# A new hand-written order, engine choice and memory map for two layers of state-space model and two of long convolution, on one core

## The chip, the cores and the metric

The kernel runs on one core of a Trainium2 chip. A core has TensorE (PE, matrix products, with a separate row for its weight loads, PEld), VectorE (DVE), ScalarE (ACT), GpSimd (POOL) and SyncE (SP). Every engine takes its instructions in the order in which they were written for it, and waits for others through semaphores. Products land in PSUM, eight banks of 512 fp32 columns on 128 partitions; everything else lives in SBUF. Transfers are issued from the SP queue, and the first small parameters from ScalarE's.

The metric is the device time of one execution in microseconds. Before the change three runs took 341.73 to 342.29 us, median 342.02.

## What is computed

Four residual layers in turn on `x`, 2048 tokens of 640 features, bf16 in and out: A, B, A, B. A normalizes, runs a diagonal complex recurrence and projects back. B normalizes and multiplies with a long convolution of `kv`. The weights are the same in both A layers, and `k`, `v` and the filter the same in both B layers.

```python
def _A_ref(x, ...):                       # x is the layernorm of the stream
    Lam_bar = jnp.exp(dt * Lam)           # 640 complex poles
    B_bar = ((Lam_bar - 1.0) / Lam)[:, None] * Bmat
    Bu = jnp.einsum("bld,pd->blp", x + 0j, B_bar)
    for t in range(L):
        h = Lam_bar[None, :] * h + Bu[:, t, :]
    y = 2.0 * jnp.einsum("blp,dp->bld", hseq, Cmat).real + x * Dskip
def _B_ref(q, k, v, shift_k, ssm_k, ssm_D):
    kv = k_shift * v                      # k_shift: 4 taps over time
    y = irfft(rfft(pad(kv)) * rfft(pad(ssm_k)))[:S] + kv * ssm_D
    return q * y
x = x + A(ln(x)); x = x + B(ln(x)); x = x + A(ln(x)); x = x + B(ln(x))
```

## The kernel before

**Tasks and their order.** The program is cut into 896 named tasks. Each has a function that emits its instructions, the tasks it depends on, and one or two engines that can do it. The text `ORDER` names every task once; `Sched.run` walks through it and emits one task after the other. So the order in the text, filtered by engine, is the order of each engine's queue. A suffix `/a`, `/d` or `/p` picks ScalarE, VectorE or GpSimd where a task has a choice; without one it runs on its first engine. `PLACE` gives every SBUF buffer its offset in one arena (in units of 64 bytes per partition, 3216 of them) and every product its PSUM bank. A buffer that lies where another lay before makes its writer wait until the earlier users are done.

**Convolution tables and kv.** `yt_*` make sine tables (`yt_io` and `yt_f0` counters on GpSimd, `yt_ph`, `yt_f2`, `yt_neg` on VectorE, `yt_sin`, `yt_f3` on ScalarE; `yt_Ci`, `yt_Si` are transposes by DMA). `kv_*` make the shifted product: small parameters come by `kv_kd`, `kv_dsl` (and `a_pl` for layer A) on ScalarE's queue, `kv_k0`, `kv_d0` and `a_p0` cast them (L1164, L1178, L359), `kv_ds` build diagonal matrices on GpSimd, `kv_lk` and `kv_lv` load k (transposed) and v, `kv_mm` is the product (L1227), `kv_ev` multiplies by v (L1243, VectorE), `kv_pd` fills 16 columns with zeros.

**Convolution, five groups of 128 features (`yq0` to `yq4`).** The filter (`kl`, stages `KA`, `KB`) and kv (`vl`, a transpose by DMA, stages `VA`, `VB`) are transformed by products (`:m`, L1272 and L1294 to L1296) that are evicted from PSUM by a copy (`:e`, ScalarE L290 or VectorE L292). `pw` multiplies the spectra on VectorE (L1350 to L1354), `IB` (L1376), a DMA transpose `tt` and `IA` (L1404) go back, and `st` writes the result to a scratch in HBM, from which `B1l` and `B2l` read it.

**Layer A's weights.** `a_ldB`, `a_ldC` load, `a_b0`, `a_b1`, `a_ct`, `a_w1` are products, `a_b0e`, `a_b1e`, `a_wc`, `a_wm`, `a_w1e` their evictions. `a_p*`, `a_t*`, `a_f`, `a_dd`, `a_lm2`, `a_lamd`, `a_tq` and `a_rq` make poles, rotation tables and diagonals. Two neighbouring tokens (four in the last chunk) are taken as one step of the recurrence.

**Layers, four chunks of 512 tokens.** For `A1c0` to `A2c3`: layernorm statistics (`ln_bn` on VectorE in A1, `ln_sq` on ScalarE elsewhere), normalization (`id`, ScalarE L696 or VectorE L698), a transpose by DMA (`tu`, L726), input products `bq` (L750) and `bp` (L765) in three groups with evictions `eq` and `ev`, then on VectorE a rotation `ri` (L803, L804), the scan `sc` (L820), the carry `cy` to the next chunk, and the rotation back `ro`. `hx` (L875) takes away the input again for the even tokens. Four output products `cp:0` to `cp:3` (L901) follow; `cp:1` and `cp:3` need `ro` alone, `cp:0` and `cp:2` need `hx` as well. `xe` adds the residual (VectorE L911, or ScalarE L909, where an identity product has added it). The last chunk has further steps: `e2`, `b4` (L781, L783) before the rotation, `h1` (L858 to L861), `eh` and two `hx` behind it. `B1` and `B2`: normalization `u`, product `mm` (L959), sum `m` (L980, L982), in B2 with a store `st`. B2's last chunk goes by single quarters (`B2c30` to `B2c33`, L944, L948).

The scans carry from chunk to chunk, and each chunk goes through A1, B1, A2, B2, so the chunks run staggered, with the convolution groups and the weights in between.

Of the kernel before, what the change touches and what calls it, by code (L numbers as in the profile page):

```python
# [59 lines left out]
a_ldB1 yt_io8 kv_pd0/p yt_ph8 a_ldB0 yq0_kl kv_kd kv_dsl a_pl yt_f0 yt_h0 kv_k0 kv_pd1/p kv_lk0 kv_lv0 yq1_kl yt_sin8  # L60
xl0 kv_lk1 kv_lv1 yt_f2 kv_pd2/d yt_f3 a_p0 a_ti yt_io0 yt_ph0 yt_f4 kv_d0 yt_neg8 yt_h1 warm a_p1 a_p2 yt_sin0
a_b00:3 a_b0e0:3/d a_b01:2 a_b00:2 kv_k1 kv_k2 yq0_ka a_b01:3 a_b0e1:2/a a_p3 a_b0e0:2/d a_b0e1:3/d a_b00:1 yq0_KA:m0
a_b00:4 a_p4a yq0_KA:e0/a a_dd yt_neg0 kv_d1 kv_d2 kv_ds0 kv_ds4 kv_ds1 yq0_KA:m3 a_p5a a_b0e0:1/a a_b0e0:4/d
yq0_KA:e3/a a_b01:0 yq0_KA:m2 a_b0e1:0/a a_b00:0 yq0_KA:m1 yq0_KA:e2/a a_p4 yq0_KA:e1/d a_b0e0:0/d a_ta kv_mm0:1
a_b01:4 a_p5b a_b0e1:4/a yt_h2 kv_ds2 kv_ds3 yt_h3/p kv_mm0:0 kv_ev0:1 kv_pd3/d yq1_ka yq1_KA:m1 yq0_KB:m2 yq0_KB:m0
yq1_KA:e1/a yq0_KB:e2/a a_t0 kv_ev0:0 A1c0_ln_bn:1/d a_p6 a_lamd/d kv_pd4/p a_f yq0_vl a_ldC0 yt_Ci a_ldC1 yq0_KB:e0/a
yt_Si kv_lv3 kv_lk2 kv_lv2 xl2 yq2_kl yq1_KA:m3 yq1_KA:m2 yq0_KB:m3 yq1_KA:e2/a yq0_KB:e3/a kv_mm1:0 yq1_KA:e3/a
a_b01:1 a_b0e1:1/d kv_ev1:0 kv_mm1:1 kv_ev1:1 a_t1 a_b11:3 a_b1e1:3/d yq0_VA:m2 a_b11:0 yq0_VA:e2/d A1c0_ln_bn:2/d
a_b1e1:0/d a_b10:1 a_b11:1 a_b1e0:1/a a_b1e1:1/a yq0_KB:m1 yq0_KB:e1/a yq0_VA:m1 a_b11:4 a_lm2 a_b1e1:4/d yq0_VA:m3
yq0_VA:e1/a yq0_VA:m0 yq0_VA:e0/a yq0_VA:e3/d yq1_KA:m0 yq1_KA:e0/a a_b10:4 a_b1e0:4/a yq0_VB:m0 a_ct1 yq0_VB:e0/a  # L70
a_wc01:0 A1c0_ln_bn:3/d yt_nci A1c0_ln_bn:0/d a_t2 yq0_VB:m3 yq0_VB:e3/a yq0_VB:m2 a_b10:2 yq0_VB:e2/a a_wm01:0 yt_nsi
# [1488 lines left out]
```

## Time and profile before

| | us |
|---|---|
| median of three runs | 342.02 |
| the profiled execution, its own time | 342.43 |
| its span, first to last instruction | 340.6 |
| VectorE busy | 320.2 (94%) |
| TensorE busy / weight loads | 309.3 (91%) / 241.8 |
| ScalarE busy | 245.1 (72%) |
| GpSimd busy | 18.1 (5%) |
| granted TensorE clock, mean | 0.979 |
| DMA: moved, mean rate | 41.61 MB, 122 GB/s |

A busy time is the union of an engine's instructions. Matmuls overlap in it, since their ends are modelled: a mean of 273 ns stands beside starts that are 109 ns apart. Evictions from PSUM and normalizations are split between VectorE and ScalarE: of the copies of 1024 columns 111 run on ScalarE and 27 on VectorE. An "idle before" is the time that the engine stood before an instruction, with the engine or transfer whose signal ended it.

### The profile page before, as it was taken

The page shows a single profiled execution, that of the slowest core. Times are in us where ns is not written, and L with a number is a line of the kernel's source. Part 1 is how long each engine was busy: PE and PEld are TensorE (multiplying, and loading weights), DVE is VectorE, ACT ScalarE, POOL GpSimd, SP SyncE. Part 2 cuts the span into 40 slices and gives each one's busy share as a digit, 9 for nine tenths or more (in the row PEclk, how much of TensorE's full clock was granted, in tenths as well). Part 3 has the DMA queues.
Part 4 walks back from the last instruction along what each step waited for, and adds up shares of the span by engine and source line. Part 5 has one row for each costly group of instructions (what it writes and reads, how often), then busy time and mean ns, then how long its engine had stood idle before and what let it go on. Part 6 is the DMA issues. An engine that isn't in the chain of part 4 may idle for free. (4 is left out here: it accounts for less than half of the span.)

```text
span 340.6 us, 8904 instructions
## 1 busy us (share of the span) xinstructions
PE 309.3 (91%) x3817; PEld 241.8 (71%) x3838; DVE 320.2 (94%) x485; ACT 245.1 (72%) x389; POOL 18.1 (5%) x52
## 2 busy tenths in 40 slices
PE   6676978967899999999999999999999899999991
PEld 2566877866788989888676678686676686775650
DVE  5999998999998699999999999999999999999995
ACT  4899987989787867774596589887385793264772
POOL 6590000000000000000000000000000000000000
PEclk9789999997999999999999999999999999999997
DMA  8988999999959293159009460624001260008013
GB/s 234 238 173 180 204 248 228 130 222 214 156 125 187 64 155 72 39 90 239 29 2 187 122 252 2 157 77 79 0 2 25 55 154 2 2 1 306 27 56 154
DMA packets 105097, 41.61 MB, mean 122 GB/s; under 512 B 97885, under 2 KB 100450, under 8 KB 105058
## 3 DMA queue, kind: packets, MB, share of 16 engines
q1 hardware_dynamic: 104912, 41.03, 56.2%
q8 instruction: 30, 0.49, 0.6%
q14 instruction: 9, 0.07, 0.1%
q10 hardware_dynamic: 146, 0.01, 0.0%
HBM read 19.02 MB, written 5.24 MB: 71 GB/s over the span
## 5 line engine op out<-in xcount | busy, mean ns | idle before, releaser
L290 ACT ACTIVATE arena<-banks 128x1024 bf16<-128x1024 f32 (+3 forms) x151 | 130.1, 911 | 54.8 <-PE banks L750 17.3
L901 PE MATMUL banks<-arena 128*128 128x128 bf16 (+1 forms) x780 | 98.2, 281 | 1.1
L901 PEld LDWEIGHTS <-arena 128*128 128x128 bf16 x800 | 59.7, 98 | 39.9 <-issue 1.7
L750 PE MATMUL banks<-arena 128*128 128x256 bf16 x400 | 46.3, 273 | 1.1 <-DVE arena L911 1.1
L765 PE MATMUL banks<-arena 128*128 128x256 bf16 x400 | 46.5, 273 | 0.0
L292 DVE CAST arena<-banks 128x1024 bf16<-128x1024 f32 (+3 forms) x39 | 41.1, 1078 | 5.5 <-PE banks L1404 2.4
L644 ACT ACTIVATE junk<-arena,sums 128x640 bf16<-128x640 f32 x48 | 39.6, 825 | 5.2 <-DVE arena L911 2.5
L750 PEld LDWEIGHTS <-arena 128*128 128x128 bf16 x400 | 38.3, 98 | 5.7 <-DMA arena<-arena 1.2
L765 PEld LDWEIGHTS <-arena 128*128 128x128 bf16 x400 | 38.4, 98 | 4.4
L803 DVE TENSOR_TENSOR arena<-arena 128x5160 bf16<-128x5160 bf16 (+1 forms) x16 | 40.2, 2510 | 0.3
L820 DVE TENSOR_TENSOR_SCAN arena<-arena 128x1290 bf16<-128x1290 f32 (+1 forms) x16 | 39.3, 2500 | 0.2
L1294 PE MATMUL banks<-arena 128*128 128x256 bf16 x160 | 38.2, 279 | 1.4 <-ACT arena L290 1.1
L1295 PE MATMUL banks<-arena 128*128 128x128 bf16 x160 | 35.6, 222 | 0.0
L1296 PE MATMUL banks<-arena 128*128 128x128 bf16 x160 | 35.6, 222 | 0.0
L696 ACT ACTIVATE arena<-arena,nmr,rstd 128x640 bf16<-128x640 f32 (+1 forms) x31 | 26.9, 911 | 3.9 <-DVE nmr L657 3.9
L1376 PE MATMUL banks<-arena 128*128 128x128 bf16 (+1 forms) x288 | 24.0, 237 | 1.4 <-DVE arena L493 1.0
L1376 PEld LDWEIGHTS <-arena 128*128 128x128 bf16 x288 | 20.8, 98 | 3.3 <-issue 1.5
L911 DVE SCALAR_TENSOR_TENSOR arena<-banks,arena 128x640 f32<-128x640 f32 x27 | 21.8, 818 | 0.5 <-issue 0.4
L804 DVE TENSOR_TENSOR arena<-arena 128x2580 bf16<-128x2580 bf16 (+1 forms) x16 | 21.4, 1337 | 0.6
L1296 PEld LDWEIGHTS <-arena 128*128 128x128 bf16 x160 | 16.0, 100 | 2.2
L1295 PEld LDWEIGHTS <-arena 128*128 128x128 bf16 x160 | 15.9, 100 | 1.8 <-issue 1.7
L1294 PEld LDWEIGHTS <-arena 128*128 128x128 bf16 x160 | 15.9, 100 | 1.2 <-DVE arena L292 0.2
(210 smaller groups left out, 411.5 us busy)
## 6 DMA issues: line engine op xcount, KB each, us to landing
arena<-in_A_x_dram SPq DMA_DIRECT2D x8, 640.0 KB, 5.1
arena<-ysd SPq DMA_DIRECT2D x8, 640.0 KB, 5.1
arena<-in_B_ssm_k_dram SPq DMA_DIRECT2D x5, 512.0 KB, 6.7
arena<-in_B_v_dram SPq DMA_DIRECT2D x5, 512.0 KB, 5.6
ysd<-arena SPq DMA_DIRECT2D x5, 512.0 KB, 3.8
out_dram<-arena SPq DMA_DIRECT2D x8, 320.0 KB, 2.2
arena<-in_A_B_im_dram SPq DMA_DIRECT2D x1, 800.0 KB, 4.9
arena<-in_A_B_re_dram SPq DMA_DIRECT2D x1, 800.0 KB, 6.9
```

What stands on the lines that cost most here:

```text
L290: nc.scalar.activation(out, in_, ACT.Copy)
L292: nc.vector.tensor_copy(out, in_)
L644: nc.scalar.activation(small.junk, src(q), ACT.Square, bias=sums()[:, i:i + 1], scale=-float(D), accum_out=st["ssq"][:, i:i + 1])
L750: nc.tensor.matmul(pb[:, jj, c2, :], lhsT=bt0[:, c2, k, j * P:(j + 1) * P], rhs=uT[:, 2:4, k, :], start=(c2 == k == 0), stop=(c2 == 1 and ...
L765: nc.tensor.matmul(pb[:, jj, c2, :], lhsT=bt1[:, c2, j, k, :], rhs=uT[:, 0:2, k, :], start=False, stop=(c2 == 1 and k == NJ - 1), skip_gro ...
L803: nc.vector.tensor_tensor(tt, gs[:, :, None].to_broadcast([P, 2, 2, n]), by_pairs(tab.get().rearrange("p i j b -> p (i j b)"), n), ALU.mult)
L820: nc.vector.tensor_tensor_scan(gv, rt, gv, 0.0, ALU.mult, ALU.add)
L901: nc.tensor.matmul(pc[:, o0:o1], lhsT=lh, rhs=rh, start=(n == 0), stop=(n == len(ops) - 1))
L1294: nc.tensor.matmul(ps[:, g], lhsT=T["Cf"].get()[:, q, :], rhs=A[:, 2 * q:2 * q + 2, :], start=True, stop=False, skip_group_check=True)
L1295: nc.tensor.matmul(ps[:, g, 0, :], lhsT=T["Sf"].get()[:, q, :], rhs=aim, start=False, stop=False, skip_group_check=True)
L1296: nc.tensor.matmul(ps[:, g, 1, :], lhsT=T["NSf"].get()[:, q, :], rhs=are, start=False, stop=True, skip_group_check=True)
L1376: nc.tensor.matmul(ps[:, bi + b0:bi + b1, :], lhsT=T[tb].get()[:, q, :], rhs=rh, start=(n == 0), stop=(n == len(ops) - 1), skip_group_chec ...
```

## The change

Only the two texts are new. `ORDER` names the same 896 tasks in another sequence, and 71 of them with another engine; `PLACE` has the same 416 names with other offsets and banks.

From VectorE to ScalarE (39): `A1c0_id:0,3`, `A1c1_id:2,3`, `A1c2_id:0`, `A1c3_id:2`, `A2c1_id:1,2`, `A2c2_id:1,3`, `B1c0_u:0,3`, `B1c1_u:0`, `B1c3_u:2`, `B2c0_u:3`, `B2c2_u:1`, `A1c1_eq:0`, `A2c1_ev:0`, `A1c3_e2:1,2`, `A1c3_xe:1`, `a_b0e0:0,2,3,4`, `a_b0e1:1`, `a_tq`, and twelve evictions of the convolution (`yq0_KA:e1`, `yq0_VB:e1`, `yq0_IB:e2`, `yq0_IA:e1`, `yq1_IB:e3`, `yq2_IB:e2`, `yq3_KB:e1`, `yq3_VB:e0`, `yq4_KA:e2`, `yq4_VB:e1`, `yq4_VB:e3`, `yq4_IB:e1`).

From ScalarE to VectorE (29): `A1c1_ln_bn:1`, `A1c1_id:1`, `A2c0_id:0,1`, `A2c1_id:0`, `B1c0_u:2`, `B1c1_u:1`, `B1c2_u:0,1`, `B1c3_u:3`, `B2c0_u:0`, `B2c2_u:3`, `A1c3_eq:1,2`, `A1c3_ev:2`, `A1c3_xe:0`, `A2c3_eh:2`, `a_b1e0:1`, and eleven of the convolution (`yq0_KA:e0`, `yq0_KA:e2`, `yq0_KB:e1`, `yq2_VB:e0`, `yq2_VB:e1`, `yq2_VB:e3`, `yq2_IB:e0`, `yq2_IB:e1`, `yq3_VA:e3`, `yq3_VB:e2`, `yq4_VA:e3`). Three `kv_pd` move between VectorE and GpSimd.

Transfers on the SP queue, from `yq0_vl` to `yq1_tt`. Before: `yq0_vl a_ldC0 yt_Ci a_ldC1 yt_Si kv_lv3 kv_lk2 kv_lv2 xl2 yq2_kl xl1 yq1_vl kv_lk3 yq2_vl yq0_tt kv_lk4 yq3_kl xl3 A1c0_tu yq0_st kv_lv4 yq3_vl yq1_tt`. After: `yq0_vl a_ldC0 xl2 a_ldC1 yq2_kl yt_Ci kv_lk2 yt_Si kv_lv2 xl1 yq1_vl kv_lk3 kv_lv3 yq2_vl yq0_tt xl3 A1c0_tu yq3_vl kv_lk4 yq3_kl kv_lv4 yq0_st yq1_tt`. Further on, before: `A1c1_tu yq1_st A1c2_tu yq2_tt yq2_st A1c3_tu`, and `B1l3 A2c1_tu A2c2_tu A2c3_tu B2l0 B2c0_st:1 B2l1 B2l2`; after: `A1c1_tu A1c2_tu yq1_st A1c3_tu yq2_tt`, and `B2l1 A2c1_tu B1l3 A2c2_tu B2l2 A2c3_tu B2l0`. GpSimd's queue, before: `yt_io8 kv_pd0 yt_f0 yt_h0 kv_pd1 a_ti yt_io0 yt_h1 a_dd kv_ds0 kv_ds4 kv_ds1 kv_ds2 kv_ds3`; after: `yt_io8 a_ti yt_h0 yt_io0 kv_pd2 yt_f0 kv_pd0 kv_ds0 kv_ds1 a_dd yt_h1 kv_ds4 kv_ds3 kv_ds2`.

The diff, cut to the first stage, the place of `A1c0_tu` and `A1c0_bq:2`, the end of the scans, and the first line of the places:

```diff
 ORDER = """
-a_ldB1 yt_io8 kv_pd0/p yt_ph8 a_ldB0 yq0_kl kv_kd kv_dsl a_pl yt_f0 yt_h0 kv_k0 kv_pd1/p kv_lk0 kv_lv0 yq1_kl yt_sin8
-xl0 kv_lk1 kv_lv1 yt_f2 kv_pd2/d yt_f3 a_p0 a_ti yt_io0 yt_ph0 yt_f4 kv_d0 yt_neg8 yt_h1 warm a_p1 a_p2 yt_sin0
-a_b00:3 a_b0e0:3/d a_b01:2 a_b00:2 kv_k1 kv_k2 yq0_ka a_b01:3 a_b0e1:2/a a_p3 a_b0e0:2/d a_b0e1:3/d a_b00:1 yq0_KA:m0
-a_b00:4 a_p4a yq0_KA:e0/a a_dd yt_neg0 kv_d1 kv_d2 kv_ds0 kv_ds4 kv_ds1 yq0_KA:m3 a_p5a a_b0e0:1/a a_b0e0:4/d
-yq0_KA:e3/a a_b01:0 yq0_KA:m2 a_b0e1:0/a a_b00:0 yq0_KA:m1 yq0_KA:e2/a a_p4 yq0_KA:e1/d a_b0e0:0/d a_ta kv_mm0:1
-a_b01:4 a_p5b a_b0e1:4/a yt_h2 kv_ds2 kv_ds3 yt_h3/p kv_mm0:0 kv_ev0:1 kv_pd3/d yq1_ka yq1_KA:m1 yq0_KB:m2 yq0_KB:m0
-yq1_KA:e1/a yq0_KB:e2/a a_t0 kv_ev0:0 A1c0_ln_bn:1/d a_p6 a_lamd/d kv_pd4/p a_f yq0_vl a_ldC0 yt_Ci a_ldC1 yq0_KB:e0/a
-yt_Si kv_lv3 kv_lk2 kv_lv2 xl2 yq2_kl yq1_KA:m3 yq1_KA:m2 yq0_KB:m3 yq1_KA:e2/a yq0_KB:e3/a kv_mm1:0 yq1_KA:e3/a
-a_b01:1 a_b0e1:1/d kv_ev1:0 kv_mm1:1 kv_ev1:1 a_t1 a_b11:3 a_b1e1:3/d yq0_VA:m2 a_b11:0 yq0_VA:e2/d A1c0_ln_bn:2/d
...
-a_wc00:1 a_wm00:1 yq1_pw:0 yq0_IA:e0/a A1c0_tu yq0_st kv_lv4 yq3_vl yq2_VA:m2 yq2_VA:e2/a yq2_VA:m1 yq2_VA:m3
...
-yq2_VB:e3/a yq2_VB:e2/d A1c1_id:3/d A1c3_ln_sd yq3_KA:e2/a A1c0_bq:2 kv_mm4:0 yq3_KA:m1 A1c0_eq:2/a A1c3_ln_post
...
-A2c2_cy A2c1_xe:2/d B2c0_mm B2c0_m:0 A2c2_ro B2c0_m:3 A2c2_hx B2c0_m:2 B2c0_m:1 B2c1_ln_sq:2 B2c1_ln_sq:3 A2c3_eq:0/a
-A2c3_bp:0 A2c3_ev:2/a B2c1_ln_sq:1 A2c3_e2:1/a B2c0_st:1 B2l1 A2c3_b4:1 A2c3_e2:0/a A2c3_ev:1/a B2c1_ln_sq:0
-B2c1_ln_sd B2l2 B2c0_st:3 A2c2_cp:1 B2l3 B2c1_ln_post A2c2_xe:1/d A2c3_b4:0 A2c3_ev:0/a A2c3_ri A2c2_cp:3 A2c2_xe:3/d
-A2c3_sc A2c3_ro A2c3_hx:1 B2c1_u:0/a B2c1_u:3/a B2c1_u:2/a B2c1_u:1/a A2c2_cp:2 A2c2_xe:2/d B2c1_mm B2c1_m:2 B2c1_m:1
-B2c1_m:3 B2c1_m:0 A2c2_cp:0 A2c2_xe:0/a B2c2_ln_sq:2 A2c3_h1:0 A2c3_h1:2 A2c3_h1:1 A2c3_eh:1/a B2c2_ln_sq:1
-A2c3_eh:2/a A2c3_eh:0/a B2c2_ln_sq:0 B2c2_ln_sq:3 B2c2_ln_sd A2c3_cp:3 A2c3_xe:3/d B2c1_st:1 B2c1_st:3 A2c3_cp:2
-A2c3_hx:0 B2c2_ln_post B2c2_u:1/d B2c33_ln_nm B2c33_u:3 B2c33_ln_sq:3 A2c3_xe:2/d B2c33_ln_sd B2c2_u:0/a B2c2_u:2/a
-B2c33_ln_post B2c33_m:3 B2c32_ln_nm B2c32_u:2 A2c3_cp:0 B2c2_u:3/a B2c2_mm B2c2_m:2 B2c2_m:1 B2c2_m:3 B2c32_ln_sq:2
-A2c3_xe:0/a B2c30_ln_nm B2c30_u:0 B2c2_m:0 A2c3_cp:1 B2c32_ln_sd B2c30_ln_sq:0 B2c32_ln_post B2c30_ln_sd B2c32_m:2
-B2c30_ln_post B2c30_m:0 A2c3_xe:1/a B2c31_ln_nm B2c31_ln_sq:1 B2c31_ln_sd B2c2_st:1 B2c3_st:3 B2c2_st:3 B2c31_u:1
...
+a_ldB1 a_ldB0 yt_io8 yt_ph8 kv_dsl kv_kd yq0_kl a_pl a_ti yt_h0 yt_io0 kv_pd2/p yt_f0 kv_lk0 kv_k0 yt_ph0 yt_f2 kv_d0
+kv_lv0 warm kv_k1 a_b01:2 yt_sin8 xl0 yq1_kl kv_lk1 a_p0 kv_lv1 yt_sin0 yt_f3 a_b0e1:2/a a_p1 a_b00:4 a_b00:2 yt_neg8
+kv_pd4/d kv_k2 yt_f4 kv_pd0/p a_p2 yq0_ka a_b0e0:4/a a_b01:3 yq0_KA:m0 a_b0e0:2/a a_p3 a_b00:3 a_b0e1:3/d yq0_KA:e0/d
+kv_pd3/d kv_d1 kv_d2 a_p4a a_p4 kv_ds0 kv_ds1 a_dd yt_h1 kv_ds4 kv_ds3 kv_ds2 a_b00:1 a_b0e0:3/a a_b0e0:1/a a_b01:0
+yt_neg0 a_b0e1:0/a a_b00:0 a_b0e0:0/a yq0_KA:m3 yq0_KA:e3/a yq0_KA:m2 kv_mm0:1 yq0_KA:e2/d kv_pd1/d a_ta yq0_KA:m1
+a_b01:4 yq0_KA:e1/a kv_mm0:0 a_b0e1:4/a kv_ev0:1 a_t0 kv_ev0:0 yq0_vl a_ldC0 xl2 a_ldC1 a_p5a a_p5b yq0_KB:m0
+yq0_KB:e0/a yq0_KB:m2 yq2_kl yt_Ci kv_lk2 yq0_KB:e2/a yt_Si a_p6 kv_lv2 yq1_ka a_f A1c0_ln_bn:1/d a_lamd/d yq1_KA:m1
...
+yq1_VB:e3/d A1c2_id:1/d xl3 A1c0_tu yq1_VB:e0/a a_wc00:0 yq1_VB:m2 yq0_IA:m1 yq1_VB:e2/a yq0_IA:m0 yq3_vl kv_lk4
...
+yq2_VB:m0 yq2_VB:m3 yq2_VB:m2 yq2_VB:e0/d yq2_VB:e3/d yq3_KA:m2 A1c0_bq:2 A1c3_ln_post yq2_VB:e2/d yq3_KA:e2/a
...
+A2c2_sc B2c0_u:0/d A2c1_xe:3/d A2c2_cy A2c1_cp:2 A2c3_bp:2 A2c1_xe:2/d A2c3_bq:0 B2c1_ln_sq:1 A2c3_e2:2/a A2c3_bp:1
+A2c3_b4:2 B2c1_ln_sq:3 A2c3_eq:0/a B2c1_ln_sq:0 B2c1_ln_sq:2 A2c3_ev:2/a B2c1_ln_sd A2c3_e2:1/a A2c2_ro B2c0_mm
+B2c0_m:3 A2c3_bp:0 A2c2_cp:1 B2c1_ln_post B2c1_u:1/a A2c3_e2:0/a A2c3_b4:1 A2c3_b4:0 B2c1_u:0/a B2c1_u:2/a B2c1_u:3/a
+B2c0_m:1 B2c0_m:0 A2c2_hx B2c0_m:2 A2c2_cp:0 B2c0_st:1 B2l3 B2c0_st:3 A2c3_ev:0/a A2c3_ev:1/a A2c2_xe:1/d B2c1_mm
+A2c2_cp:2 A2c3_ri A2c3_sc A2c3_ro A2c2_xe:0/a A2c2_cp:3 A2c3_h1:1 A2c3_eh:1/a B2c1_m:3 A2c2_xe:2/d A2c3_h1:0
+A2c3_eh:0/a A2c3_h1:2 A2c3_cp:3 A2c2_xe:3/d B2c2_ln_sq:2 B2c2_ln_sq:0 B2c2_ln_sq:1 B2c2_ln_sq:3 B2c2_ln_sd B2c1_m:0
+A2c3_eh:2/d B2c1_m:1 A2c3_hx:1 A2c3_hx:0 A2c3_cp:2 A2c3_cp:0 A2c3_xe:3/d B2c1_m:2 A2c3_cp:1 B2c2_ln_post B2c2_u:3/d
+B2c33_ln_nm B2c33_u:3 B2c33_ln_sq:3 B2c33_ln_sd B2c2_u:2/a B2c2_u:1/a A2c3_xe:2/d B2c33_ln_post B2c33_m:3 B2c32_ln_nm
+B2c2_u:0/a B2c32_u:2 B2c2_mm B2c2_m:0 B2c2_m:2 B2c2_m:1 B2c2_m:3 B2c1_st:3 B2c32_ln_sq:2 B2c2_st:1 B2c2_st:3
...
 """
...
-    "par": 3037, "yCf": 1214, "ySf": 64, "yNSf": 663, "yCi": 1150, "ySi": 2016, "yNSi": 292, "ytmp0": 727,
...
+    "par": 751, "yCf": 2016, "ySf": 1219, "yNSf": 1155, "yCi": 64, "ySi": 289, "yNSi": 680, "ytmp0": 2907,
...
```

## Prediction, made before the result was known

> **What bounds the kernel now.** I read the stages first: the busy time of every engine in stretches cut where the character of the work changes. The columns are the stretch, then busy us and instruction counts of PE, weight loads, VectorE (DVE), ScalarE (ACT) and GpSimd, then granted clock, DMA share and GB/s.
>
> ```profile
> 0.00:8.50 8.50, 5.62 (x18) 2.08 (x18) 4.40 (x29) 3.48 (x5) 5.84 (x25) 1.00 0.81 234
> 8.50:96.70 88.20, 70.38 (x1450) 61.42 (x1450) 83.54 (x163) 77.71 (x106) 12.28 (x27) 0.94 1.06 201
> 96.70:119.00 22.30, 21.92 (x360) 19.27 (x356) 18.49 (x21) 17.95 (x25) 0.00 (x0) 1.00 0.58 111
> 119.00:305.85 186.85, 184.57 (x1790) 142.56 (x1803) 183.21 (x227) 127.07 (x213) 0.00 (x0) 1.00 0.36 79
> 305.85:340.60 34.75, 26.81 (x213) 16.52 (x213) 30.55 (x49) 18.87 (x42) 0.00 (x0) 0.94 0.37 133
> ```
>
> To 96.7 us VectorE is busy 83.54 of 88.20 us, ScalarE 77.71, TensorE 70.38: the two engines that empty PSUM set the pace. From 96.7 to 305.85 TensorE is busy 206.49 of 209.15 us and VectorE 201.70. Both are full, and what is taken off one of them there doesn't shorten it. The last 34.75 us is a chain.
>
> [...] If TensorE had headroom, every microsecond taken from VectorE would count, and its whole relief (7.6 us, below) would come out: 334.4 us. So I counted: from 119.0 to 331.5 us the groups by shape hold some 321 matmuls of 512 columns, 838 of 256 and 667 of 128, with a few small ones. [...] The engine is really full, and I take nothing for that stretch.
>
> Then the waits of the first stage, from the timelines of VectorE, ScalarE and the SP queue (start, duration, instruction, in brackets the idle time before it and what ended it):
>
> ```profile
> 8.50 0.21 DVE L359 CAST arena<-arena 20x128 f32<-20x128 bf16 x1 [2.44 <-DMA arena<-in_A_Dskip_dram]
> 8.64 0.47 DVE L1022 TENSOR_SCALAR arena<-arena,pidx 128x512 int32<-128x512 f32 x1
> 9.14 0.43 DVE L1023 TENSOR_SCALAR arena<-arena 128x512 int32<-128x512 int32 x1
> ```
> ```profile
> 9.60 0.72 ACT L1030 ACTIVATE arena<-arena,neg_pi 128x512 bf16<-128x512 int32 x1 [2.85 <-DVE arena L1023]
> ```
> ```profile
> 19.20 0.58 SPq L1198 DMA_DIRECT2D arena<-in_B_v_dram  x1
> 25.74 1.94 SPq L1329 DMA_TRANSPOSE arena<-arena  x1
> ```
>
> VectorE stood 2.44 us for the small parameters with yt_ph0 and kv_d0 queued behind; ScalarE's yt_sin0 waited 2.85 us for yt_ph0. The first kv transpose leaves the SP queue at 25.74 us, after a gap that compute made.
>
> **The change, part by part.** Work, sizes and dependencies are the same; three things differ.
>
> *Engines.* 68 tasks change between VectorE and ScalarE, three 16-column fills with GpSimd. The rows for the sizes:
>
> ```profile
> L290 ACT ACTIVATE arena<-banks 128x1024 bf16<-128x1024 f32 x111 | 108.8, 1026 | 40.6 <-PE banks L750 17.0 <-PE banks L765 6.5 <-PE banks L1296 5.4
> L292 DVE CAST arena<-banks 128x1024 bf16<-128x1024 f32 x27 | 32.3, 1216 | 5.4 <-PE banks L1404 2.4 <-PE banks L1272 1.2 <-PE banks L1296 1.1
> L696 ACT ACTIVATE arena<-arena,nmr,rstd 128x640 bf16<-128x640 f32 x28 | 24.3, 911 | 3.9 <-DVE nmr L657 3.9
> L698 DVE TENSOR_SCALAR arena<-arena,rstd,nmr 128x640 bf16<-128x640 f32 x16 | 9.4, 609 | 0.1
> L292 DVE CAST arena<-banks 128x640 bf16<-128x640 f32 x10 | 8.0, 812 | 0.1
> ```
>
> Off VectorE go 14 evictions of 1024 columns (17.0), 5 of 640 (4.1), 10 normalizations from fp32 (6.1), 6 from bf16 at 0.44 (2.6), a_tq 2.2, two small evictions 1.1 and one residual add 0.9: 34.0. Onto it come 12 of 1024 (14.6), 10 from fp32 (6.1), one from bf16 (0.4), one of 640 (0.8), the A1c1 statistics 1.15, a residual add 0.9 and three small ones 1.5: 25.5. That is -8.5 by the rows; successive instructions overlap by about 0.08 us, and with each at its start-to-start cost I get -7.6 on VectorE and +7.7 on ScalarE. TensorE's sum doesn't change (the xe:0/xe:1 swap in A1c3 moves one pair of identity matmuls).
>
> *Order in the first stage.* A good place to compare is A1c0_bq:2, which started at 96.72 us: in both orders exactly the same TensorE tasks stand in front of it. VectorE has 92.5 us of work ahead of that place in the order before and 88.3 after: 15 tasks went to ScalarE, 8 came from it, and yq2_VB:e2 (1.15) now stands behind. So -4.2. ScalarE has 76.3 before and 79.3 after: +3.0. Besides, the parameters' cast a_p0 now stands behind yt_ph0, yt_f2 and kv_d0. VectorE from 1.94 us: yt_ph8 1.1, kv_k0 0.5 (its parameter, now issued second on ScalarE's queue, lands some 0.5-1 us later than the 3.4 us of before), yt_ph0 0.85, yt_f2 2.45, kv_d0 0.35, so to about 8.2-8.5, when the parameters land: 0.85 + 0.35 = 1.2 us of the wait is filled. yt_sin0 follows yt_sin8 at once, which takes away ScalarE's 2.85.
>
> The limits for the arrival at that place: if VectorE alone sets it, 4.2 + 1.2 = 5.4 us earlier. If ScalarE sets it, 3.0 more work less 2.85 less waiting, 0.15 later. VectorE is the fuller by 5.8 us in the second stretch, but ScalarE gets near it, and every handover between them stays. I take the middle: **2.7 us earlier**.
>
> *The SP and GpSimd queues.* On SP, A1c0_tu goes ahead of lk4 and kl3, which held the queue for 2.84 and 0.57 us; xl2 and kl2 pass the table transposes; later B2l1 passes A2c1_tu, B1l3 goes behind it, B2l2 passes A2c3_tu. A load that waits for its place would hold the transposes behind it, so I looked whose room B2l1 takes: A1c2's, last used by A1c2_ro, long done. Cost 0. A1c2_tu and A1c3_tu go ahead too, under 226 us of TensorE work. On GpSimd, yt_h1 (3.0) and a_dd (2.9) go behind ds0 and ds1, which feed the first kv product: part of the gain above, not counted again. yt_f0 goes behind three fills, and yt_f2 behind yt_ph0 covers it; without that cover it costs at most 1.0.
>
> *From there on.* Up to A2c3_b4:0 TensorE again has exactly the same tasks ahead in both orders. Its idle there is 2.66 us from 96.7 to 305.85. The room for each chunk's rotation and scan (TensorE work between its last input product and its first output product, less VectorE's work from ri to the end of ro) grows: A1c1 4.8 to 8.4 us, A2c0 4.4 to 8.5, A2c1 6.9 to 8.4, A2c2 5.9 to 6.6; only the even tokens' room in A2c2 shrinks, 10.3 to 5.2. *Places* also move: a product waits for the eviction that last used its PSUM bank, at worst 1.2 us each time. So a gain of up to 2.7, a loss if one place starves: I take 0.
>
> *The end.* This is the chain:
>
> ```profile
> 306.49 0.60 ACT L290 ACTIVATE arena<-banks 128x512 bf16<-128x512 f32 x1 [1.64 <-PE banks L783]
> 307.27 1.51 DVE L803 TENSOR_TENSOR arena<-arena 128x2600 bf16<-128x2600 bf16 x1
> 315.27 0.84 DVE L804 TENSOR_TENSOR arena<-arena 128x1300 bf16<-128x1300 bf16 x1
> 316.47 0.27 PE L858 MATMUL banks<-arena,ident_bf 128*128 128x256 bf16 x1
> 333.00 0.70 ACT L909 ACTIVATE arena<-banks 128x640 f32<-128x640 f32 x1 [1.83 <-PE banks L901]
> ```
>
> b4:0 ends, ev:0 takes 0.6, ri, sc, ro end at 316.1, TensorE works 16.2 us through the h1 and cp products, and from the last xe to the last byte it is 7.6. After: A2c2_xe:3 (0.74) no longer lies between ri and sc, -0.7; ev:1 now comes behind ev:0, +0.5. In front of hx:1 stand six other tasks, 4.15 us, while TensorE has 2.0 of h1 and 3.2 of cp:3 first, so hx:1, done 4.9 after ro, is in time for cp:2 by 0.3. Sum 0 (-0.2 to +1).
>
> **Sum.** The profiled execution spans 340.6 us of its own 342.43; the median is 342.02. -2.7 for the first stage, 0, 0: span 337.9, and against the median 342.0 - 2.7 = **339.3 us**.
>
> **Rivals.** (a) *VectorE alone sets the first stage, and the wider rooms save stalls:* -5.4 and about -1 of the 2.66: **335.6**. For it: VectorE's 95% there. Against: ScalarE at 88% with 3 us more. (b) *Transfers set the first stage, so the change does nothing:* DMA share 1.06 to 96.7 us and an SP queue almost without a gap from 25.7 to 60: **342.0**. Against: the queue itself waited for VectorE before 25.74, and of the waits of VectorE only some 3.5 us end at a DMA. (c) *Slower: ScalarE becomes the bound of the first stage.* Its waits there are for others' products; if they stay as long as they were, apart from the 2.85, its extra work stands on the path. At the last kv product, which began at 91.0 us, 76.6 us of ScalarE work lie ahead, against 69.8. 6.8 - 2.85 = 4.0 later: **346.0**. It decides once ScalarE's idle time up to there doesn't fall below 91.0 - 76.6 = 14.4 us; it was 21.2. Against: much of it is waits for evictions that now come sooner.
>
> **How the numbers follow.** Forecast 0.45, (a) 0.27, (b) 0.09, (c) 0.19. Within 0.2% (0.7 us, about what a measurement can tell) falls most of (b), and little else: 0.08. Faster 0.45 + 0.27, less its edge and plus part of (b): 0.72. Slower, (c) and the edge of (b): 0.20. The range leaves 2 in 10 out: from 334.5, a us below (a), to 343.8, above (b) and the near half of (c). The forecast's own range is 337.5 to 341.0.
>
> **What would show it.** Right: a_p0 with under 1.5 us of wait before it and yt_sin0 starting before 7.5 us; A1c0_bq:2 at 93 to 95 us; TensorE idle 2 to 4 us from there to the end chain; VectorE about 312 us busy, ScalarE 252. Wrong: A1c0_bq:2 at 96.5 or later (b, c), with ScalarE waits then shifted to VectorE or TensorE; or a TensorE gap over 2 us past 100 us, at A2c2's or A2c3's even tokens, which would give the gain back.

## The result, and the profile after

The kernel after takes **339.23 us** (median of six, 338.67 to 340.30), beside 341.91 us for the kernel before (six, 341.25 to 342.29). The ratio is 0.9925, with a 95% interval of 0.9906 to 0.9944: faster by 0.56 to 0.94%. The forecast was 339.3. The profiled execution of after spans 337.4 of its own 339.59 us; the one of before spanned 340.6, so this pair of traces differs by 3.2, a little more than the medians.

I cut the trace of after at the same places of the work as before: the end of the start-up, `A1c0_bq:2` (93.84 us, where before had 96.72), 119, and `A2c3_b4:0` (303.14, where before had 305.85). The columns are those of the same view of before: stretch and its length, busy us and instruction counts of PE, weight loads, DVE, ACT and POOL, then granted clock, DMA share, GB/s.

```profile
0.00:8.50 8.50, 6.46 (x24) 2.68 (x24) 4.35 (x25) 4.79 (x7) 3.64 (x17) 1.00 0.83 235
8.50:93.84 85.34, 70.80 (x1448) 61.48 (x1445) 80.36 (x164) 79.98 (x109) 16.80 (x34) 0.94 1.12 207
93.84:119.00 25.16, 25.16 (x393) 21.92 (x390) 21.77 (x22) 19.12 (x25) 0.00 (x0) 1.00 0.65 132
119.00:303.14 184.14, 181.50 (x1755) 139.74 (x1770) 175.99 (x222) 132.50 (x219) 0.00 (x0) 1.00 0.35 85
303.14:337.40 34.26, 26.99 (x213) 16.48 (x213) 30.64 (x48) 16.99 (x40) 0.00 (x0) 0.96 0.26 89
```

Read the left column first. The second stretch is 2.86 us shorter than the 88.20 of before, and ScalarE is busy in it for as long as VectorE (79.98 and 80.36; before 77.71 and 83.54). Between `A1c0_bq:2` and `A2c3_b4:0` lie 209.30 us, beside 209.15 before, with TensorE idle for 0.00 + 2.64 us, beside 2.66. The last stretch is 34.26, beside 34.75. Of the 3.2 us between the two traces 2.9 are there by `A1c0_bq:2`, and the middle keeps them. The 0.5 at the end lie behind the last normalization (4.52 us from its start to the end of the span, then 4.09). They look like spread and not like a gain: a run below that ends in the order of before has 4.15 there.

The groups that the change resizes (line, engine, shapes, count, busy us, mean ns, idle time ahead of them and what ended it):

```profile
L290 ACT ACTIVATE arena<-banks 128x1024 bf16<-128x1024 f32 x113 | 110.9, 1025 | 27.1 <-PE banks L1272 7.6 <-PE banks L750 5.0 <-DVE arena L911 4.4
L292 DVE CAST arena<-banks 128x1024 bf16<-128x1024 f32 x25 | 30.1, 1219 | 3.7 <-PE banks L1296 2.6 <-PE banks L1272 0.8 <-PE banks L1404 0.2
L696 ACT ACTIVATE arena<-arena,nmr,rstd 128x640 bf16<-128x640 f32 x28 | 24.2, 912 | 12.0 <-DVE nmr L657 12.0
L698 DVE TENSOR_SCALAR arena<-arena,rstd,nmr 128x640 bf16<-128x640 f32 x16 | 9.1, 608 | 0.1
L292 DVE CAST arena<-banks 128x640 bf16<-128x640 f32 x6 | 4.8, 816 | 0.4 <-PE banks L524 0.2
```

The 1024-column evictions went from 111 and 27 to 113 and 25, at unchanged means. In front of ScalarE's there are now 27.1 us of idle time, where before had 40.6. In front of its normalizations there are 12.0, where there were 3.9.

The start, on VectorE (start, duration, instruction; in brackets the idle time before it and what ended it):

```profile
5.96 0.17 DVE L1164 CAST arena<-arena 80x8 f32<-80x8 bf16 x1 [2.83 <-DMA arena<-in_B_ssm_D_dram]
6.04 0.48 DVE L1022 TENSOR_SCALAR arena<-arena,pidx 128x512 int32<-128x512 f32 x1
...
9.25 0.41 DVE L1178 CAST arena<-arena 5x512 f32<-5x512 bf16 x1
9.59 0.21 DVE L359 CAST arena<-arena 20x128 f32<-20x128 bf16 x1
```

and on ScalarE and on the SP queue:

```profile
7.01 0.72 ACT L1030 ACTIVATE arena<-arena,neg_pi 128x512 bf16<-128x512 int32 x1
```
```profile
22.81 2.94 SPq L1329 DMA_TRANSPOSE arena<-arena  x1
```

The wait of 2.44 us in front of `a_p0` (L359) is gone, and one of 2.83 us stands in front of `kv_k0` (L1164), because its parameter landed at about 5.9 us. `yt_ph0` (L1022) is behind it. ScalarE's `yt_sin0` starts at 7.01 instead of 9.60, with no wait. The first kv transpose leaves at 22.81 instead of 25.74.

The end chain, from the timelines of ScalarE, VectorE and TensorE, again answering to the rows of before:

```profile
303.93 1.21 ACT L290 ACTIVATE arena<-banks 128x512 bf16<-128x512 f32 x2
304.43 1.49 DVE L959 TENSOR_TENSOR arena<-arena 128x2560 bf16<-128x2560 bf16 x1
305.97 1.51 DVE L803 TENSOR_TENSOR arena<-arena 128x2600 bf16<-128x2600 bf16 x1
...
313.36 0.84 DVE L804 TENSOR_TENSOR arena<-arena 128x1300 bf16<-128x1300 bf16 x1
313.76 0.27 PE L858 MATMUL banks<-arena,ident_bf 128*128 128x256 bf16 x1
```

The start of `ri` is taken at its first instruction, a short fill (L807) 0.1 us ahead of the L803 that is shown. It comes 2.73 us after `b4:0` instead of 1.32. The two 512-column evictions now stand together and end 2.00 us after `b4:0` instead of 1.24. But VectorE isn't free then: the order of after has `B2c1_mm` (L959) ahead of `ri`, where before had it behind `ro`. From `ri` to `ro` it is 5.94 us instead of 6.56. `A2c3_cp:3` starts 12.66 us after `b4:0` (before 12.58), and the last normalization `B2c31_m:1` 30.17 after it (before 30.23).

### The profile page after: what moved, and what is told of

Its sections match the earlier page's. It is cut to its first block, busy times and chain, and to the rows that moved or that the text cites. A ratio compares the mean times of both kernels' runs of the same rounds, so it can differ in the third digit from the quotient of the medians.

```text
span 337.4 us, 8902 instructions
## 1 busy us (share of the span) xinstructions
PE 310.9 (92%) x3819; PEld 242.3 (72%) x3838; DVE 313.1 (93%) x477; ACT 253.4 (75%) x396; POOL 20.4 (6%) x51
## 5 line engine op out<-in xcount | busy, mean ns | idle before, releaser
L290 ACT ACTIVATE arena<-banks 128x1024 bf16<-128x1024 f32 (+3 forms) x156 | 134.2, 910 | 43.7 <-PE banks L765 10.7
L750 PE MATMUL banks<-arena 128*128 128x256 bf16 x400 | 46.5, 273 | 1.4 <-ACT arena L290 1.4
L765 PE MATMUL banks<-arena 128*128 128x256 bf16 x400 | 46.5, 273 | 0.0
L1294 PE MATMUL banks<-arena 128*128 128x256 bf16 x160 | 39.7, 286 | 1.4 <-ACT arena L290 0.9
L803 DVE TENSOR_TENSOR arena<-arena 128x5160 bf16<-128x5160 bf16 (+1 forms) x16 | 40.2, 2511 | 0.5
L696 ACT ACTIVATE arena<-arena,nmr,rstd 128x640 bf16<-128x640 f32 (+1 forms) x36 | 31.3, 915 | 12.0 <-DVE nmr L657 12.0
L292 DVE CAST arena<-banks 128x1024 bf16<-128x1024 f32 (+3 forms) x34 | 35.9, 1085 | 4.1 <-PE banks L1296 2.6
L1295 PE MATMUL banks<-arena 128*128 128x128 bf16 x160 | 36.3, 227 | 0.0
L1296 PE MATMUL banks<-arena 128*128 128x128 bf16 x160 | 36.2, 227 | 0.0
L804 DVE TENSOR_TENSOR arena<-arena 128x2580 bf16<-128x2580 bf16 (+1 forms) x16 | 21.4, 1337 | 0.5
```

The costliest lines, as they stand in the source:

```text
L290: nc.scalar.activation(out, in_, ACT.Copy)
L292: nc.vector.tensor_copy(out, in_)
L750: nc.tensor.matmul(pb[:, jj, c2, :], lhsT=bt0[:, c2, k, j * P:(j + 1) * P], rhs=uT[:, 2:4, k, :], start=(c2 == k == 0), stop=(c2 == 1 and ...
L765: nc.tensor.matmul(pb[:, jj, c2, :], lhsT=bt1[:, c2, j, k, :], rhs=uT[:, 0:2, k, :], start=False, stop=(c2 == 1 and k == NJ - 1), skip_gro ...
L803: nc.vector.tensor_tensor(tt, gs[:, :, None].to_broadcast([P, 2, 2, n]), by_pairs(tab.get().rearrange("p i j b -> p (i j b)"), n), ALU.mult)
L1294: nc.tensor.matmul(ps[:, g], lhsT=T["Cf"].get()[:, q, :], rhs=A[:, 2 * q:2 * q + 2, :], start=True, stop=False, skip_group_check=True)
```

## The experiments

Four kernels were run beside the kernel before, whose median on that chip was 342.63 us (eleven, 342.39 to 343.47). All four compute the whole of the reference. Three change only engines in `ORDER`, and one swaps two loads. I follow them by when a few tasks started in the profiled executions (us):

| task | before | after | first-stage engines back | first-stage engines alone | later engines back | `kv_kd` first |
|---|---|---|---|---|---|---|
| `kv_d2` (VectorE) | 15.19 | 13.20 | 13.38 | 16.50 | 13.24 | 12.35 |
| `kv_mm0:1` (TensorE) | 18.23 | 15.42 | 18.62 | 18.99 | 15.99 | 14.57 |
| `kv_ev0:0` (VectorE) | 24.50 | 21.51 | 25.75 | 25.82 | 21.55 | 20.91 |
| `kv_mm1:1` (TensorE) | 29.83 | 28.20 | 33.04 | 31.46 | 27.50 | 29.30 |
| `A1c0_bq:2` (TensorE) | 96.72 | 93.84 | 107.81 | 106.25 | 93.14 | 94.94 |
| from `kv_mm1:1` to `A1c0_bq:2` | 66.89 | 65.64 | 74.77 | 74.79 | 65.64 | 65.64 |
| `A2c3_b4:0` (TensorE) | 305.85 | 303.14 | 317.10 | 315.62 | 342.18 | 304.23 |
| from `A1c0_bq:2` to `A2c3_b4:0` | 209.13 | 209.30 | 209.29 | 209.37 | 249.04 | 209.29 |

**The first stage's engines put back, in the order of after.** Of the 71 tasks with another engine, the 26 that lie ahead of `A1c0_bq:2` get the engine that they had before. Order and places stay. In short:

```diff
-... a_b0e0:4/a ... a_b0e0:2/a ... yq0_KA:e0/d ... a_b0e0:3/a ... a_b0e0:0/a ... A1c1_ln_bn:1/d ... yq0_IB:e2/a ...
+... a_b0e0:4/d ... a_b0e0:2/d ... yq0_KA:e0/a ... a_b0e0:3/d ... a_b0e0:0/d ... A1c1_ln_bn:1/a ... yq0_IB:e2/d ...
```

> The changed kernel with the engines of before for the 26 tasks that changed them ahead of A1c0_bq:2 (order and places stay). VectorE gets 15 tasks back and gives 8: by the start-to-start costs +3.4 us ahead of A1c0_bq:2, ScalarE -3.6. If VectorE's work sets the first stage: A1c0_bq:2 at 96.5 to 97.5 us and the whole back at 342 us, all of the gain lost. If ScalarE's earlier start or the order of the transfers made the gain: 339.2 or a little less.

Measured: 352.68 us (351.77 to 355.35), ratio 1.0301 (1.0274 to 1.0329), some 10 us above the slower of the two expectations. Its trace says where the time went. One line each from the timelines of TensorE, ScalarE and VectorE:

```profile
16.64 1.23 PE L508 MATMUL banks<-ident_bf,arena 128*128 128x128 bf16 x10 [2.72 <-DVE arena L292]
```
```profile
63.20 0.74 ACT L675 ACTIVATE junk<-arena 128x640 bf16<-128x640 bf16 x1 [2.67 <-DVE mv L672]
```
```profile
71.82 1.23 DVE L292 CAST arena<-banks 128x1024 bf16<-128x1024 f32 x1 [5.37 <-issue]
```

At 16.64 TensorE (`a_b01:0`) has waited 2.72 us for the eviction `a_b0e0:3`. In after that one runs on ScalarE at 13.23. Back on VectorE it has the place in the queue that `ORDER` gives it, which is behind `a_p4`, 2.2 us of small instructions, so it runs at 15.78. `kv_d2` is hardly later than in after (13.38), so its early start comes from the order and not from these evictions. `kv_mm0:1` is 3.2 us later all the same, because TensorE was held.

The other two lines are one story. `A1c1_ln_bn:1`, back on ScalarE, waits 2.67 us for VectorE, with the evictions of `yq0_IB` behind it. And `yq0_IB:e2`, back on VectorE, waits until its product has been made at 71.7, for 5.37 us in which VectorE does nothing. (That product took 3.54 us, from 68.19 on, where before and after took 1.94; the granted clock was 0.50 from about 68.3 to 71.7. More on this below.) From `A1c0_bq:2` on, this kernel takes what after takes (next experiment but one), so its whole loss is made in the first stage.

**The same 26 engines alone, in the order of before.** The mirror image of it: the kernel before, with only the engines of after for those tasks.

```diff
-... a_b0e0:3/d ... a_b0e0:2/d ... yq0_KA:e0/a ... yq0_IB:e2/d ... A1c1_ln_bn:1/a ...
+... a_b0e0:3/a ... a_b0e0:2/a ... yq0_KA:e0/d ... yq0_IB:e2/a ... A1c1_ln_bn:1/d ...
```

> The kernel before with the changed kernel's engines for the same 26 tasks alone (order and places of before). If VectorE's work sets the first stage: up to 3.4 us faster, 338.6, rather 340 since the moved evictions don't stand at places meant for their new engine. If the early order makes the gain: 342, or slower, since ScalarE still waits 2.85 us for yt_ph0 and has 3.6 us more to do.

Measured: 352.14 us (352.08 to 353.44), ratio 1.0285 (1.0269 to 1.0301). "Or slower" had been allowed for, but not 10 us. VectorE has less to do and stands idle for it. This is its timeline:

```profile
68.72 1.22 DVE L292 CAST arena<-banks 128x1024 bf16<-128x1024 f32 x1 [4.51 <-PE banks L1272]
```

From 64.21 to 68.72 VectorE has nothing in front of `yq1_VA:e0`. `yq0_IB:e2`, which it would have done then, is now one of three evictions that ScalarE does one after the other from 66.22 to 69.07.

The two runs give one answer. The order of after with the engines of before takes 74.77 us from `kv_mm1:1` to `A1c0_bq:2`, the order of before with the engines of after 74.79, and the matched pairs take 66.89 and 65.64. **Neither half carries the gain, and each without the other costs about 10 us.** So no share of the 2.7 us can be put down to "engines" or to "order" (the sequence with its places, which were not taken apart), and a theory that adds up the work per engine can't foretell a kernel in which the two don't fit.

Another thing differs in these traces: for stretches of some microseconds TensorE's granted clock falls to 0.50, half of full. The windows' rows from `kv_mm1:1` to `A1c0_bq:2`, of before, of after, of the first run and of the second (columns as in the section on the result, the clock is the third number from the right):

```profile
29.83:96.72 66.89, 55.23 (x1112) 48.69 (x1111) 63.27 (x114) 58.45 (x74) 0.00 (x0) 0.97 1.09 204
28.20:93.84 65.64, 56.64 (x1110) 49.89 (x1109) 61.11 (x108) 61.73 (x77) 2.71 (x8) 0.95 1.10 206
33.04:107.81 74.77, 59.92 (x1111) 52.44 (x1110) 62.74 (x113) 60.05 (x77) 0.32 (x1) 0.91 0.93 175
31.46:106.25 74.79, 57.99 (x1112) 51.16 (x1111) 61.17 (x111) 62.56 (x76) 0.00 (x0) 0.93 0.96 184
```

Set against the kernel with the same order, TensorE stands idle 5.9 us longer in the first run and 5.1 in the second, and is busy 3.3 and 2.8 us longer, at a lower clock. How much of this slowness comes of the waits, and how much makes new ones, the runs don't show. The loss doesn't hang on it: one execution of the first run had a mean clock of 0.978, like the traces of before (0.979) and after (0.980), and took 352.03 us.

**The later engines put back.** After, with the engines of before for the other 45 tasks, all behind `A1c0_bq:2`.

```diff
-... A1c0_ro A1c0_hx A1c1_eq:0/a ... A1c2_ri A1c2_sc ... yq4_IB:m1 yq4_IB:e1/a ...
+... A1c0_ro A1c0_hx A1c1_eq:0/d ... A1c2_ri A1c2_sc ... yq4_IB:m1 yq4_IB:e1/d ...
```

> The changed kernel with the engines of before for the 45 tasks that changed them behind A1c0_bq:2. VectorE gets some 4 us more work in the stretch where TensorE is full. If TensorE bounds that stretch and VectorE has room: 339.2, within 0.7. If VectorE's relief there was part of the gain, or its work the hidden bound: up to 4 us slower, 343.

Measured: 381.24 us (380.37 to 382.79), ratio 1.1130 (1.1110 to 1.1149), where 339.2 to 343 had been expected. Its first stage is that of after, and all 39.7 us of the loss up to `A2c3_b4:0` are in the stretch behind it. The windows' rows of that stretch, of after and of this run:

```profile
93.84:303.14 209.30, 206.66 (x2145) 161.66 (x2158) 197.76 (x243) 151.61 (x243) 0.00 (x0) 1.00 0.38 90
93.14:342.18 249.04, 218.46 (x2146) 166.73 (x2159) 202.66 (x248) 147.51 (x237) 0.00 (x0) 0.94 0.32 76
```

TensorE's idle time grew from 2.6 to 30.6 us, and 23.5 of these are waits that a VectorE eviction ended. The other 11.8 us of the loss are busy time at a lower clock (0.94, from 1.00). Two lines of TensorE's timeline, and VectorE's ahead of the second:

```profile
126.31 1.04 PE L1272 MATMUL banks<-FA,arena 64*128 64x128 bf16 x16 [4.76 <-DVE arena L292]
...
198.71 1.86 PE L901 MATMUL banks<-arena 128*128 128x512 bf16 x4 [10.40 <-DVE arena L292]
```
```profile
187.08 2.85 DVE L803 TENSOR_TENSOR arena<-arena 128x5160 bf16<-128x5160 bf16 x1
...
191.96 5.58 DVE L820 TENSOR_TENSOR_SCAN arena<-arena 128x1290 bf16<-128x1290 f32 x2
197.46 1.20 DVE L292 CAST arena<-banks 128x1024 bf16<-128x1024 f32 x1
```

At 126.31 TensorE has waited for `yq4_KA:e2`, which on VectorE stands behind `yq3_pw` (118.12 to 125.04). The wait that ends at 198.71 is the clearest case. `yq4_IB:e1` is some 1.0 us of work on ScalarE and 1.2 on VectorE. In the order of after it is named behind `A1c2_ri` and `A1c2_sc`. On ScalarE that means nothing; on VectorE it means 10.4 us of rotation and scan in front of it (187.08 to 197.46), and TensorE stands 10.40 us for its bank. In the order of before it was named ahead of `A1c2_ri`, ran on VectorE at 173.63, and TensorE had no wait for it.

The run shows a second thing. TensorE's stretch of 209 us is full only while both orders hand it its banks in time. That it is full in after is a property of this pairing, not a floor under any list of engines.

The first two runs serve here as controls. In them TensorE arrives at `A1c0_bq:2` 14.0 us later than in after and 9.5 later than in before, and from there to `A2c3_b4:0` they take 209.29 and 209.37 us, where their own later parts took 209.30 (after) and 209.13 (before). The windows' rows from `A1c0_bq:2` to `A2c3_b4:0`, of the first and of the second:

```profile
107.81:317.10 209.29, 206.65 (x2145) 161.66 (x2158) 196.93 (x240) 151.75 (x244) 0.00 (x0) 1.00 0.38 90
```
```profile
106.25:315.62 209.37, 206.59 (x2140) 161.88 (x2157) 202.11 (x246) 143.85 (x235) 0.00 (x0) 1.00 0.39 82
```

VectorE is busy 5.2 us less in the one than in the other and the time is the same. The relief of VectorE behind `A1c0_bq:2` is worth nothing, as the forecast took it.

**The first small parameter first.** The one start-up term that the trace of after contradicts at once: `kv_kd` is issued ahead of `kv_dsl` again, as in before, and the rest is after.

```diff
-a_ldB1 a_ldB0 yt_io8 yt_ph8 kv_dsl kv_kd yq0_kl ...
+a_ldB1 a_ldB0 yt_io8 yt_ph8 kv_kd kv_dsl yq0_kl ...
```

> The changed kernel with the two small parameter loads kv_kd and kv_dsl issued in the order of before. In the changed kernel VectorE stood 2.83 us at kv_k0 for the parameter of kv_kd, with yt_ph0 and all else behind it. With it first, kv_k0 should start at about 3.4 us instead of 5.96, and a_p0 at 8.5, when its own parameters land, instead of 9.59. If VectorE sets the first stage from its first microseconds on: 1.1 us faster, 338.1. If the path into the first stage runs through something else (loads of the weights, ScalarE): 339.2.

Measured: 340.43 us (337.88 to 341.04), ratio 0.9923 (0.9899 to 0.9946), which is after's own: the expectation without a gain held. VectorE's timeline shows that the wait did go where it should:

```profile
3.17 0.35 DVE L1164 CAST arena<-arena 80x8 f32<-80x8 bf16 x1
...
8.74 0.21 DVE L359 CAST arena<-arena 20x128 f32<-20x128 bf16 x1 [1.51 <-DMA arena<-in_A_Dskip_dram]
```

`kv_k0` runs at 3.17 with no wait, and at `a_p0` 1.51 us are left of one: the layout that the forecast had in mind. `a_p0` is 0.85 us earlier than in after, and so is `kv_mm0:1`. Then 1.1 us of lateness appear by `kv_mm1:1` and stay to the end. The granted clock points to where they come from. Rows of three windows (columns as above) of after, of the run with the later engines back, whose program is after's up to `A1c0_bq:2`, and of this run:

```profile
12.00:19.00 7.00, 4.56 (x133) 3.76 (x132) 6.86 (x19) 6.99 (x13) 5.56 (x12) 1.00 1.33 255
...
20.00:24.00 4.00, 3.18 (x29) 2.71 (x29) 3.86 (x14) 3.40 (x10) 3.32 (x9) 0.57 1.18 233
24.00:26.50 2.50, 2.25 (x47) 1.74 (x46) 2.40 (x9) 2.23 (x4) 2.50 (x6) 1.00 1.20 121
```
```profile
12.00:19.00 7.00, 6.43 (x117) 5.55 (x115) 6.86 (x19) 6.80 (x13) 5.52 (x12) 0.51 1.28 255
...
20.00:24.00 4.00, 2.96 (x58) 2.37 (x50) 3.86 (x13) 3.95 (x11) 3.33 (x9) 1.00 1.17 234
24.00:26.50 2.50, 2.30 (x83) 1.93 (x79) 2.40 (x9) 2.50 (x4) 2.50 (x6) 1.00 1.17 114
```
```profile
12.00:19.00 7.00, 4.50 (x166) 3.71 (x166) 6.86 (x19) 6.99 (x14) 6.41 (x13) 1.00 1.13 251
...
20.00:24.00 4.00, 3.49 (x30) 2.91 (x30) 3.65 (x16) 2.62 (x5) 3.39 (x10) 0.50 1.14 246
24.00:26.50 2.50, 2.50 (x28) 1.92 (x27) 2.47 (x5) 1.94 (x2) 2.50 (x5) 0.50 1.32 78
```

TensorE runs at half clock once in this part of these three traces, but not at the same place: from 12.1 to 18.9 us in the run with the later engines back, from 20.3 to 23.7 in after, from 19.7 to 26.5 here. From `kv_ev0:0` to `kv_mm1:1` these three take 5.95, 6.69 and 8.39 us. In this run's last window TensorE is busy for all 2.50 us, at half clock. So I put down to the half clock about 0.7 us in after, and about 2.4 in this run, as against the one that had it earlier. That is 1.7 more than in after: a lead of 0.6 us at `kv_ev0:0` becomes the 1.1 behind. This is read from one trace of each. In the medians the two kernels can't be told apart, and the six times of this run lie 3.2 us apart, those of before on the same chip 1.1. The clock doesn't order these times: the execution with the highest mean clock of the six, 0.992, took 339.84 us, one with 0.990 took 337.88. Why the 0.85 us don't show in the median stays open.

## Why the prediction was right, step by step

**The first stage, -2.7: right in its sum, for partly other reasons.** `A1c0_bq:2` came at 93.84, 2.88 us earlier and inside the 93 to 95 that were named. Busy time up to that place, by the windows of before and of after, shows how:

```profile
0.00:96.72 96.72, 76.02 (x1468) 63.51 (x1469) 87.96 (x191) 81.22 (x111) 18.12 (x52) 0.95 1.04 204
```
```profile
0.00:93.84 93.84, 77.26 (x1468) 64.16 (x1468) 84.71 (x188) 84.77 (x115) 20.44 (x51) 0.95 1.09 209
```

VectorE is busy 3.25 us less and idle 0.37 us more (8.76, then 9.13): -3.25 + 0.37 = -2.88. ScalarE is busy 3.55 more and idle 6.43 less (15.50, then 9.07), the same -2.88. Set against the steps:

- *VectorE's work ahead of that place, -4.2.* The sign and most of the size held. 3.25 is busy time cut by the clock and not by the place in the order, so the two differ by what VectorE had already done of the work behind.
- *The wait for the small parameters, -1.2 filled.* **This step failed.** The parameter of `kv_k0`, issued second, was taken to land 0.5 to 1 us later than at 3.4. It landed at about 5.9, 2.6 later, and the wait moved from `a_p0` to `kv_k0` instead of shrinking: 2.44, then 2.83 us. VectorE's idle time in the stage did not fall. With this term at nothing, the two limits were -4.2 and +0.15, and their middle -2.0; the near agreement of 2.7 with 2.88 owes something to this error. The run with `kv_kd` first shows what the step had been worth: 0.85 us at `a_p0`, and nothing that the medians show.
- *ScalarE's wait of 2.85 us goes.* It did: `yt_sin0` at 7.01, under the 7.5 named.
- *The middle between the two engines.* Neither limit came true. As VectorE gave up 3.25 us of work and the arrival gained 2.88, the case is nearer to "VectorE alone" than to the middle. But ScalarE ended as busy as VectorE (84.77 and 84.71 us), and the first two experiments show the arrival set by which hand-over stands in front of which. I didn't run a kernel that adds work to one engine and keeps the order, so which of the two would pay for the next microsecond stays open.

The pair of traces carries the half clock as well. In the run with the later engines back, whose half clock lay where it did in before (12.1 to 18.9 there too, and 3.4 us more near 80), `A1c0_bq:2` came at 93.14: 3.58 us earlier than in before. So 2.88 is probably the gain less some 0.7 us of clock.

**SP and GpSimd, 0.** No trace contradicts it. `A1c0_tu` left SP at 70.54 instead of 75.57, and `yq1_tt`, behind it in both orders, 2.9 us earlier. No kernel that undoes only these moves was run, so the zero is consistent with the traces, not shown.

**From `A1c0_bq:2` to `A2c3_b4:0`, 0.** Shown: 209.13 us became 209.30, and 209.29 and 209.37 with arrivals 14.0 and 9.5 us later. The wider rooms for the scans saved nothing, as there was nothing to save: TensorE's idle time was 2.64 us, inside the 2 to 4 named. That TensorE has no room, the starts in the trace of before bear out: between 119.0 and 331.5 us a matmul of 512, 256 or 128 columns starts 216, 109 or 56 ns (medians) ahead of the next, and 321, 838 and 667 of them at these distances come to 198 of the 212.5 us, smaller and fp32 ones to 8 more. The places cost nothing that shows. The 1.2 us named as the worst wait for a bank were the author's estimate, from the length of an eviction: the run with the later engines back stood 10.40 us at one.

**The end, 0.** From `b4:0` to the last normalization 30.23 became 30.17 us. The two terms came with their signs: +1.41 up to `ri` (+0.5 had been taken, for two evictions in a row), -0.62 from `ri` to `ro` (-0.7). Of the +1.41 the evictions make 0.76. The other 0.65 are `B2c1_mm` ahead of `ri`, which the forecast overlooked. Of their +0.8 only 0.08 is left at `A2c3_cp:3`, since TensorE began the identity matmul (L858) only 0.4 us behind VectorE's L804, where in before it came 1.2 behind. So this zero is in part luck.

**The rivals.** "VectorE alone and saved stalls" (335.6) named the right engine, and added 1.2 us of filled wait and 1 us of stalls that didn't come. "Transfers set it" (342.0) fell: the stage became shorter with a DMA share of 1.12 instead of 1.06 in its long part. "ScalarE becomes the bound" (346.0) asked that ScalarE's idle time up to the last kv product not fall below 14.4 us. The forecast had 21.2 for it in before by the order; by busy time in the windows it went from 14.65 (to 91.05) to 7.59 (to 88.17). ScalarE's waits were for products that came sooner, and shrank. The whole busy times were forecast as 312 and 252 and are 313.1 and 253.4.

## What to carry to other kernels

In a kernel whose engines each work through a queue in one written order, an eviction's engine and its place are one choice: moved to the other engine alone, 1.2 us of work stood behind 10.4 us of rotation and scan and held TensorE for all of it. So cost such a move by what lies in front of it in the queue that it enters, and not by its busy time; sums of busy time are good for a limit on a change in which both fit, and say nothing of one in which they don't. And read what a stage can gain from whether TensorE is idle in it: here 2.66 us of idle time in 209 said that 5 us off VectorE buy nothing.

## What the runs showed of the hardware that was not expected

**With `kv_kd` second in line, its cast came 2.5 us later and its issue only 0.6.** `kv_kd` was issued at 0.73 us in before and its cast ran at 3.46. It was issued at 1.31 in after, and the cast, which waited for nothing else, ran at 5.96: 0.6 us later in the issue, 2.5 us later at the cast. With only these two loads swapped back it ran at 3.17. In all six traces it is 3.2 to 3.5 with this load first and 5.8 to 6.0 with it second. What holds the second one isn't shown.

**The stretches at a granted clock of 0.50 were 3.4, 6.8 or 10.2 us long, and lay at other places from trace to trace.** From granted clocks in half-microsecond windows I get, up to 31 us, stretches at 0.50 of 6.8 us in before (12.1 to 18.9), 3.4 in after (20.3 to 23.7), 6.8 and 3.4 in the run with the first-stage engines back, 10.2 in the one with those engines alone, 6.8 with the later engines back and 6.8 with `kv_kd` first. Between 68 and 96 us, in windows of one microsecond, every trace has more of it, in the same sequence 3.4, 6.8, 3.4 and 10.2, 3.4 and 6.8, 3.4, 3.4. All of these are about one, two or three times 3.4 us. The program of after and that of the run with the later engines back are the same up to there, and theirs began 8 us apart (20.3 and 12.1). What starts and ends them isn't shown. The price differed with the place: by the reading above, an estimate from one trace of each, 0.7 to 2.4 us ahead of `kv_mm1:1`, nearly as much as this whole change, and nothing that shows behind it. From `kv_mm1:1` to `A1c0_bq:2` after took 65.64 us with 6.8 us of half clock, and the runs with the later engines back and with `kv_kd` first took 65.64 with 3.4.
